# Half-chunk conversion in the first dense layer of a fused attention, expert and dense kernel, with four smaller reorderings

## The chip, the cores and the metric

The program runs on one core of a Trainium2 chip. Its engines are TensorE (PE: matrix products, PEld: their weight loads), VectorE (DVE), ScalarE (ACT), GpSimd (POOL) and SyncE (SP, which here only issues transfers). The metric is the device time of one launch in microseconds (us); lower is better.

## The reference

q, k and v have the shape (4, 12, 448, 64). Three layers follow one another; `x` between them has 1792 rows of 768 numbers.

```python
scores = q @ k.T / sqrt(64) - log(448);  x = sigmoid(scores) @ v    # attention, then heads side by side
e = argmax(x @ w_gate, axis=1)                                      # 8 experts, one for each row
out[e == i] = gate[e == i] * (relu(x[e == i] @ w1[i]) @ w2[i])      # 768 -> 1024 -> 768
h = relu(out @ w_in);  result = (h * h) @ w_out                     # dense: 768 -> 2048 -> 768
```

`w_in` and `w_out` come as float64. The kernel turns them into float32 itself, with integer operations on the two 32-bit words of each number.

## The kernel before

Every float32 product is made of three products of rounded parts: a high part (ACT copies it into a rounding type) and a low part (DVE subtracts), high times high, high times low, low times high. So each weight or operand tile costs one ACT and one DVE pass before PE can use it (`split_w`, L498 and L499; `stage_high` and `stage_low`, L640 and L643; `halves`, L1110 and L1111).

The instruction order is written by hand: inside `tc.manual_schedule()` every engine runs its instructions in program order, and an instruction that waits holds back all that stand behind it on its engine. SP's transfers, which also carry all loads, stand in one such order as well.

The stages, in order of time:

- **Attention** over 24 pairs of heads, with the routing of the rows (logits, largest expert) beside it.
- **15 slots** of 128 rows each, all of one expert. `make_slot` gives `up(c)` for c = 0..3 and `down(c)` for c = 4..7, one for each weight chunk of 128x1536 numbers. After each, `next_chunk(s, c)` splits that chunk for the next slot and loads the one after. Slots 0 and 1 use the same expert, found early. The other rows' places are worked out in slot 0 by `opening(c)`: `late_places` (DVE, at c = 4) computes each row's place and then the one-hot tables `Bs` and `Bt` (L279, L281); `spots` (DVE, c = 5, 16 instructions, L223) builds `A`. In slot 1, `pick_rows` (16 small PE products, L227) multiplies both, and `late_rows` writes the row numbers by which GpSimd gathers rows. `xtrans` (c = 5 of each slot, L307 to L309) transposes the next slot's rows and splits them into `xh` and `xl`.
- **First dense layer, block 0** (rows 0 to 1023, in halves h of 512): `layer1(c, h)` for 8 chunks c, 36 PE products of 512 columns each (L1204 to L1206), in two groups `fi` of 18. ACT evicts a group by `r` (Relu, L1210) and squares it into `h` (L1213); there are two PSUM buffers. Between them `rest()` is called four times in each step (k == 2 of a group, and after it). It works through `todo`: the float64 conversion of the dense weights' chunks 9 to 15, 8 calls each. `narrow(n, step, ...)`: step 0 loads a chunk (1536 KB, L103); steps 1 to 4 are four DVE instructions over 128x1536 (L115, L117, L121, L125) and one ACT Abs (L123), which overwrites a word that the DVE instructions of steps 1 and 2 read; then the result goes to `t_d` in DRAM (L129) and the next chunk is loaded; steps 5 and 6 form four sums of 128x384 (L134 to L138) and store them (L139). When a chunk is done, `ready` lets `load_next` read `t_d` back. After steps (0, 0) and (1, 0), `trans_y` transposes the four row tiles of the second half (12 PE transposes after each, L689) out of buffers that `load_y` fills (`yn`, L666); there are two buffers, so the loads of tiles 2 and 3 go out when tiles 0 and 1 have been read. Between the steps stand the weights' splits (`advance`), `second` and `combine` (DVE sums L1218, L1219, L1075 to L1078).
- **Second dense layer, block 0**, as seven products of half-size blocks (L1383 to L1385).
- **Block 1** (rows 1024 to 1791, 768 of them): its first layer is `strassen_in`, 4 column pairs `cp` of 7 products `i` by 2 columns `ci`, 9 PE instructions each (L1267). Products of i = 0 and 1 add into one PSUM bank, as do 2 and 3, and 4 to 6; DVE or ACT reads the bank in between (L1275, L1279, L1281). The operands of i = 4, 5, 6 (blocks 6, 5 and 7) are split late, by `split_late(b)`, in the first column pair. Its second layer is again seven products; `evac` (L1359) adds the results and calls `scatter` (L1174), which writes 128 rows of the output by an indirect transfer from GpSimd. The last three scatters stand behind the loops.

Of the kernel before, what the change touches and what calls it, by code (L numbers as in the profile page):

```python
# [11 lines left out]
F32R = mybir.dt.float32r  # L12
# [3 lines left out]
U32 = mybir.dt.uint32  # L16
# [49 lines left out]
def moe_kernel(ctx: ExitStack, tc: tile.TileContext, qk, v, wg, wm, w2, out):  # L66
# [148 lines left out]
    def places(n):  # L215
        V.tensor_reduce(out=pos[:, :n], in_=posA[:, :, :n].rearrange("p e t -> p t e"), op=ALU.add, axis=AX.X)
        V.tensor_scalar(posi[:, :n], pos[:, :n], 1.0, None, op0=ALU.subtract)
        V.tensor_scalar(sli[:, :n], posi[:, :n], 7, None, op0=ALU.arith_shift_right)
        V.scalar_tensor_tensor(plf[:, :n], sli[:, :n], -128.0, pos[:, :n], op0=ALU.mult, op1=ALU.add)

    def spots(ts):
        for t in ts:
            V.tensor_scalar(A[:, t], iot1[:CP], plf[:, t:t + 1], None, op0=ALU.is_equal)  # L223
# [45 lines left out]
    def late_places(pn, prk):  # L269
        V.tensor_copy(sa[:, 2, 1:], pn)  # L270
        V.scalar_tensor_tensor(dlt, qs[:, :E], -128.0 * LSLOT, sx[:, 0, 1:], op0=ALU.add, op1=ALU.add)
        V.scalar_tensor_tensor(oh2, prk, 0.0, oh, op0=ALU.is_ge, op1=ALU.mult)
        V.scalar_tensor_tensor(posA, Sx[:CP].unsqueeze(2).to_broadcast([CP, E, NR]), 1.0, prk, op0=ALU.add, op1=ALU.add)
        V.tensor_tensor(posB, prk, sa[:CP, 0, 1:].unsqueeze(2).to_broadcast([CP, E, NR]), op=ALU.is_ge)
        V.tensor_tensor(posB, posB, dlt[:CP].unsqueeze(2).to_broadcast([CP, E, NR]), op=ALU.mult)
        V.tensor_tensor(posA, posA, posB, op=ALU.subtract)
        V.tensor_tensor(posA, posA, oh2, op=ALU.mult)
        places(NR)
        V.tensor_tensor(Bs, iot[:CP, :LC].unsqueeze(1).to_broadcast([CP, NR, LC]),  # L279
                        sli.unsqueeze(2).to_broadcast([CP, NR, LC]), op=ALU.is_equal)  # L280
        V.tensor_tensor(Bt, Bs, tokc.unsqueeze(2).to_broadcast([CP, NR, LC]), op=ALU.mult)  # L281
# [364 lines left out]

    ready = [PRE]
    cv = []
    todo = [(n, k) for n in range(PRE, 16) for k in range(1, 9)]

    def rest():
        if not todo:
            return
        n, step = todo.pop(0)
        if step < 7:
            narrow(n, step, *cv, None)
        if step == 4 and n < 15:
            narrow(n + 1, 0, cv[0], None, None)
        if step == 6:
            ready[0] = n + 1  # L660
            load_next()

# [40 lines left out]
    with ExitStack() as mctx:  # L703
# [42 lines left out]
        def make_slot(s, xh, xl, weights):  # L746
            hr = {}
            hh = mp.tile([128, KF, 128], F32R, tag="hh", name=f"hh_{s}", bufs=1)
            hl = mp.tile([128, KF, 128], F32R, tag="hl", name=f"hl_{s}", bufs=1)
            y = mp.tile([128, DM + 1], F32, tag="y", name=f"y_{s}", bufs=1)  # L750
            ps = {}

            def htrans(i):
                pt = ps_ht.tile([128, 4, 128], F32, tag="pht", name=f"pht_{s}_{i}")
                for f in range(4):
                    nc.tensor.transpose(pt[:, f, :], hr[i][:, f * 128:(f + 1) * 128], ident)
                nc.scalar.activation(hh[:, 4 * i:4 * i + 4], pt, AF.Copy)
                nc.vector.tensor_tensor(hl[:, 4 * i:4 * i + 4], pt, f32(hh[:, 4 * i:4 * i + 4]), op=ALU.subtract)

            def up(c):  # L760
                i = c // 2
                if c % 2 == 0:
                    ps[i] = ps_h.tile([128, 512], F32, tag=f"ph{i}", name=f"ph_{s}_{i}")
                w, wl_ = weights(c)
                passes(ps[i], c % 2 == 0, c % 2 == 1, ((0, 0), (1, 0), (0, 1)), 3,
                       lambda a, q: (xh, xl)[a][:, 3 * (c % 2) + q, :], lambda a, q: (w, wl_)[a][:, q * 512:q * 512 + 512],
                       (lambda: htrans(0)) if c == 2 else None)
                if c % 2 == 1:
                    hr[i] = mp.tile([128, 512], F32, tag="hr", name=f"hr_{s}_{i}", bufs=1)
                    nc.scalar.activation(hr[i], ps[i], AF.Relu)  # L770

            def down(c):
                fg, dh = (c - 4) // 2, c % 2
                if fg == 0:
                    ps[2 + dh] = ps_y.tile([128, 512], F32, tag=f"py{dh}", name=f"py_{s}_{dh}")
                w, wl_ = weights(c)
                py = ps[2 + dh][:, :384]
                passes(py, fg == 0, fg == 1, ((0, 0), (0, 1), (1, 0)), 4,
                       lambda a, q: (hh, hl)[a][:, 4 * fg + q, :], lambda a, q: (w, wl_)[a][:, q * 384:(q + 1) * 384])
                if c == 4:  # L780
                    htrans(1)

            def fin(c):
                if c > 5:
                    dh = c % 2
                    nc.scalar.activation(y[:, dh * 384:(dh + 1) * 384], ps[2 + dh][:, :384], AF.Copy, scale=gts[:, s:s + 1])
                if c == 7:
                    nc.gpsimd.tensor_copy(y[:, DM:].bitcast(U32), tok[:, s:s + 1])
                    nc.sync.dma_start(out=y_d[ds(regr[s], 128), :DM + 1] if s >= FS else y_d[128 * s:128 * s + 128, :DM + 1], in_=y)

            return up, down, fin


# [149 lines left out]
        def opening(c):  # L943
            if c == 0:
                take(4)
            elif c == 1:
                counts(pn2, prk2, NR)
                slots(pn2)
                regs(FS)
                regs(FS + 1)  # L950
                for k in (0, 1, 6, 7):
                    reload(FS, k)
            elif c == 2:
                take(5)
                take(6)
            elif c == 3:
                for k in range(2, 5):
                    reload(FS, k)
            elif c == 4:
                take(7)  # L960
                reload(FS, 5)
                late_places(pn2, prk2)
            elif c == 5:
                spots(range(NR))

        r2 = ps_q.tile([128, 512], F32, tag="q", name="r2")
# [2 lines left out]
        for s in range(NBASE):  # L969
# [10 lines left out]
                ycur.append([load_y(0, 0, t, mp.tile([128, CH], F32, tag="qraw", name=f"yr{t}", bufs=QB)[:, :DM + 1], None) for t in range(2)])  # L980
            for c in range(4):
                up(c)
                if s == 1 and c == 0:
                    pick_rows(pr2, Bt, NR)
                    late_rows(pr2)
                    for k in range(FS, FS + 2):
                        xg[k] = gather(k)
                if s == 0:
                    opening(c)
                else:  # L990
                    next_chunk(s, c)
                if s == 1 and c == 2:
                    late_sums()
                if s == FS:
                    if c == 2:
                        late_gates()
                    if c == 3:
                        more = nc.values_load(ctl[0:1, 2, NBASE:NBASE + 1], min_val=0, max_val=NT)
                q_step(s, c)
                if last:  # L1000
                    trans_y(0, 0, c, ycur[0][c], ynext, ps_x, ("px0", "px1"))
            if last:
                cv.extend(wpair(w, F32, f"{w}c") for w in ("wh", "wl"))
                narrow(PRE, 0, cv[0], None, None)
                start_ring()
            for c in range(4, 8):
                down(c)
# [147 lines left out]
        V.tensor_tensor(t3, t2, h0, op=ALU.subtract)  # L1155
        V.tensor_tensor(t3, t3, l0, op=ALU.subtract)

    def split_late(b):
        k2 = page(F32R, f"x{b}k")[:, :2 * DH]
        X[b] = [[page(F32R, f"x{b}{n}")[:, :2 * DH], k2[:, i * DH:(i + 1) * DH]] for i, n in enumerate("hl")]  # L1160
        for t in range(3):
            halves(X[b], t, late[b][t].rearrange("p (k n) -> p k n", k=3))

    def operand(b):
# [2 lines left out]
    def advance():  # L1167
        used[0] += 1
        if pos_["s"] < len(seq):
            stage(pos_["s"])  # L1170
            load_next()

    def scatter(t, ob):
        return nc.gpsimd.indirect_dma_start(out=out[:, :], out_offset=bass.IndirectOffsetOnAxis(ap=idx2[:, t:t + 1], axis=0),  # L1174
                                            in_=ob, in_offset=None)

    def quarter_rows():
        for q in range(NQ):
# [7 lines left out]
    for bi, (t0, P) in enumerate(blocks):  # L1186
# [47 lines left out]
        def strassen_in():  # L1234
# [18 lines left out]
            for cp in range(4):  # L1253
                bank = {}
                for i, o in enumerate(TURN):
                    for ci in range(2):
# [25 lines left out]
                            nc.scalar.activation(h[end], h[end], AF.Relu)  # L1282
                        if end is not None:
                            nc.scalar.activation(h[end], h[end], AF.Square)
                        if cp == 0 and (i, ci) in ((0, 1), (1, 0), (1, 1)):
                            split_late({1: 6, 2: 5, 3: 7}[2 * i + ci])
                        if (i, ci) == (0, 1) and held:
                            stage_high(held.pop())
                            late_low = True
# [127 lines left out]
                    if i < 4:  # L1417
                        parts.append(load_part((i + 2) % 3, (i + 2) // 3))
    order.close()
    sent = []  # L1420
    for p in range(P):
        st = scatter(t0 + p, obs[0][p])
        for other in sent:
            tc.declare_no_dep(st.ins, other, reason="every scatter writes rows of its own")
        sent.append(st.ins)


def layout(q, k, v, moe_w_gate, moe_w1, moe_w2, moe2_w_in, moe2_w_out):
# [45 lines left out]
```

## Time and profile before

| what | value |
|---|---|
| device time, median of 3 runs | 940.14 us (939.84 to 940.34) |
| the profiled execution's own time | 940.25 us |
| its span, first to last instruction | 938.8 us |
| mean granted TensorE clock over the span | 0.994 |
| PE, DVE, ACT, POOL busy, share of the span | 98%, 73%, 60%, 10% |

Busy means that an instruction of the engine was under way. The time is about 1.45 us more than the span. [...]

### The profile page before, as it was taken

To read this page: it belongs to the slowest core of one execution; us is meant where nothing else is said; L and a number is where in the kernel's file an instruction comes from. 1 tells how busy PE (TensorE), PEld (TensorE's weight loads), DVE (VectorE), ACT (ScalarE), POOL (GpSimd) and SP (SyncE) were. 2 spreads that over 40 slices of the span, in tenths; PEclk is the share of its full clock that TensorE was granted. 3 is DMA by queue.
4 is the path that set the end of the run, shared out by engine and by line. 5 is a ranking of instruction groups with operands and counts; after the bars stand their busy time and mean duration, and the time that the engine had idled before them with its cause. 6 is when DMAs were issued, how large, how long until landed. Compare 5 with 4: busy or idle time off the path is not lost. (4 is left out here: it accounts for less than half of the span.)

```text
span 938.8 us, 15174 instructions
## 1 busy us (share of the span) xinstructions
PE 922.3 (98%) x5803; PEld 774.7 (83%) x5803; DVE 689.8 (73%) x821; ACT 567.2 (60%) x704; POOL 98.5 (10%) x132
## 2 busy tenths in 40 slices
PE   9999999999999999999998999999999999999997
PEld 4555555589888888889987878889999999999997
DVE  3888876689876867768856797847878766569863
ACT  5767755758777777777854345445544456666541
POOL 1000001111311110101001111110000220000002
PEclk9999999999999999999999999999999999999999
DMA  8798977681787969692536787664333345456412
GB/s 289 261 368 319 336 240 247 211 312 46 247 296 266 371 242 365 231 402 98 213 148 237 268 298 245 230 251 135 103 118 118 119 158 195 135 172 236 130 35 101
DMA packets 62753, 206.36 MB, mean 220 GB/s; under 512 B 9106, under 2 KB 28690, under 8 KB 60626
## 3 DMA queue, kind: packets, MB, share of 16 engines
q1 hardware_dynamic: 42562, 159.85, 48.9%
q0 software_dynamic: 8816, 39.73, 10.9%
q10 hardware_dynamic: 11296, 5.75, 2.2%
q8 instruction: 47, 0.77, 0.3%
q14 instruction: 32, 0.26, 0.1%
HBM read 210.40 MB, written 45.63 MB: 273 GB/s over the span
## 5 line engine op out<-in xcount | busy, mean ns | idle before, releaser
L499 DVE TENSOR_TENSOR wl<-raw,wh 128x1536 fp32r<-128x1536 f32 x109 | 190.0, 1756 | 56.7 <-ACT wh L498 54.0
L498 ACT ACTIVATE wh<-raw 128x1536 fp32r<-128x1536 f32 x109 | 160.1, 1482 | 2.2 <-PE ph L732 1.9
L396 ACT ACTIVATE a<-sc,bias_s 128x896 f32<-128x896 f32 x96 | 82.6, 913 | 55.7 <-PE sc L392 55.7
L1383 PE MATMUL pq<-wrh,sh 128*128 128x384 f32 x264 | 89.0, 337 | 0.0
L1385 PE MATMUL pq<-wrh,sl 128*128 128x384 f32 x264 | 88.8, 336 | 0.0
L1384 PE MATMUL pq<-wrl,sh 128*128 128x384 f32 x264 | 88.7, 336 | 0.0
L499 DVE TENSOR_TENSOR wrl<-raw,wrh 128x1536 fp32r<-128x1536 f32 x25 | 43.8, 1756 | 22.3 <-ACT wrh L498 22.3
L498 ACT ACTIVATE wrh<-raw 128x1536 fp32r<-128x1536 f32 x25 | 37.0, 1483 | 38.2 <-PE pq L1385 38.2
L402 PE MATMUL po<-a,qkv 128*64 128x448 f32 x288 | 59.6, 548 | 0.0
L732 PE MATMUL py<-wh,hh 128*128 128x384 f32 x240 | 55.4, 352 | 0.0
L1231 DVE TENSOR_TENSOR sl<-h,sh 128x1024 fp32r<-128x1024 f32 (+1 forms) x47 | 51.6, 1111 | 4.2 <-ACT sh L1230 4.2
L732 PE MATMUL ph<-wh,xh 128*128 128x512 f32 x180 | 53.4, 405 | 0.0
L732 PE MATMUL ph<-wl,xh 128*128 128x512 f32 x180 | 52.9, 402 | 0.0
L732 PE MATMUL ph<-wh,xl 128*128 128x512 f32 x180 | 51.7, 396 | 0.8 <-DVE xl L309 0.8
L732 PE MATMUL py<-wh,hl 128*128 128x384 f32 x240 | 51.7, 337 | 0.0
L732 PE MATMUL py<-wl,hh 128*128 128x384 f32 x240 | 51.6, 336 | 0.0
L1210 ACT ACTIVATE r<-pp 128x512 f32<-128x512 f32 x32 | 19.2, 600 | 51.4 <-PE pp L1206 51.4
L1385 PEld LDWEIGHTS pq<-wrh,sl 128*128 128x128 f32 x264 | 49.5, 188 | 0.3 <-DVE sl L1231 0.3
L1384 PEld LDWEIGHTS pq<-wrl,sh 128*128 128x128 f32 x264 | 49.5, 188 | 0.0
L1383 PEld LDWEIGHTS pq<-wrh,sh 128*128 128x128 f32 x264 | 49.5, 188 | 0.0
L1230 ACT ACTIVATE sh<-h 128x1024 fp32r<-128x1024 f32 (+1 forms) x47 | 44.5, 962 | 7.6 <-PE pq L1384 6.7
L402 PEld LDWEIGHTS po<-a,qkv 128*64 128x64 f32 x288 | 18.4, 136 | 32.7 <-issue 30.6
(447 smaller groups left out, 2156.5 us busy)
## 6 DMA issues: line engine op xcount, KB each, us to landing
raw<-in_wm SPq DMA_DIRECT2D x110, 768.0 KB
qraw<-in_wm SPq DMA_DIRECT2D x32, 768.0 KB
raw<-t_d SPq DMA_DIRECT2D x28, 768.0 KB
cs<-in_w SPq DMA_DIRECT2D x9, 1536.0 KB
qkv<-in_qk SPq DMA_DIRECT2D x23, 480.0 KB
whc<-in_w SPq DMA_DIRECT2D x7, 1536.0 KB
t_d<-wlc POOLq DMA_DIRECT2D x14, 768.0 KB, 8.6
qkv<-in_v SPq DMA_DIRECT2D x24, 256.0 KB
```

The lines of the kernel that those rows point to most:

```text
L396: nc.scalar.activation(a[:, :n], ps[:, :n, :S], AF.Sigmoid, bias=bias_s, scale=1.0 / math.sqrt(D))
L402: nc.tensor.matmul(po[64 * h:64 * h + 64, :S], vr[:, 128 * c + 64 * h:128 * c + 64 * h + 64], a[:, h], start=(c == 0), stop=False, skip_gr ...
L498: nc.scalar.activation(h, src, AF.Copy)
L499: nc.vector.tensor_tensor(l, src, f32(h), op=ALU.subtract)
L732: nc.tensor.matmul(ps, left(i, q), right(j, q), start=first and a == 0 and q == 0, stop=last and a == 2 and q == n - 1)
L1210: nc.scalar.activation(r[:, :N], pp[:, :N], AF.Relu)
L1230: nc.scalar.activation(sh[:, :2 * N], src, AF.Copy)
L1231: V.tensor_tensor(sl[:, :2 * N], src, f32(sh[:, :2 * N]), op=ALU.subtract)
L1383: nc.tensor.matmul(po[p][:, :DH], lh, wc[:, w0:w0 + DH], start=(q == 0 and kk == 0 and o in (0, 2, 5)), stop=False, **fl)
L1384: nc.tensor.matmul(po[p][:, :DH], lh, wcl[:, w0:w0 + DH], start=False, stop=False, **fl)
L1385: nc.tensor.matmul(po[p][:, :DH], ll, wc[:, w0:w0 + DH], start=False, stop=(q == 3 and kk == 1), **fl)
```

## The change

- **Conversion.** `todo` has steps 0 to 7 for each chunk. Steps 0 to 2 convert the first half of the chunk's columns (768 results), 4 to 6 the second half; 3 does nothing. Step 0 or 4 issues the first two DVE instructions of a half, 1 or 5 the third and the Abs, 2 or 6 the fourth; after that the half goes to `t_d` and the same half of the next chunk is loaded (768 KB). Step 7 issues all four sums and their store, and raises `ready`. The loads of chunk 9 are two halves too.
- **Routing.** `Bs` and `Bt` move out of `late_places` into `late_picks`, which stands at c = 5 of slot 0, behind `xtrans` and ahead of `spots`. `pick_rows`, `late_rows` and two gathers move from behind `up(0)` of slot 1 to behind `up(1)`; `next_chunk(1, 0)` moves there as well. `up(0)` of slot 1 multiplies by the weights' low part second and by `xl` third; before it was the other way round.
- **Late split.** `split_late(7)` was called once, at (i, ci) = (1, 1). Now its three tiles are split one each at (2, 0), (2, 1) and (3, 0).
- **Last scatters.** Each of the last three scatters is declared independent of the three scatters before it; before, only of each other.

```diff
@@ late_places
         places(NR)
+
+    def late_picks():
         V.tensor_tensor(Bs, iot[:CP, :LC].unsqueeze(1).to_broadcast([CP, NR, LC]),
...
@@ the conversion
-    todo = [(n, k) for n in range(PRE, 16) for k in range(1, 9)]
+    todo = [(n, k) for n in range(PRE, 16) for k in range(8)]
+    HC = CH // 2
+
+    def fetch_half(n, hf):
+        src, c = cv[0], slice(hf * HC, hf * HC + HC)
+        if wide:
+            nc.sync.dma_start(out=src[:, hf * CH:hf * CH + CH].bitcast(U32), in_=w2[:, n, c].bitcast(U32))
...
+    def narrow_half(n, hf, step):
+        src, c = cv[0], slice(hf * HC, hf * HC + HC)
+        raw_ = cv[1][:, c]
+        if wide:
+            pairs = src[:, hf * CH:hf * CH + CH].rearrange("p (n two) -> p n two", two=2)
+            lo_u, hi_u = pairs[:, :, 0].bitcast(U32), pairs[:, :, 1].bitcast(U32)
+            du = raw_.bitcast(U32)
+            if step == 0:
+                nc.vector.tensor_scalar(du, hi_u, 3, 0x3FFFFFF8, op0=ALU.logical_shift_left, op1=ALU.bitwise_and)
+                nc.vector.scalar_tensor_tensor(du, hi_u, 0xC0000000, du, op0=ALU.bitwise_and, op1=ALU.bitwise_or)
+            elif step == 1:
+                nc.vector.scalar_tensor_tensor(du, lo_u, 29, du, op0=ALU.logical_shift_right, op1=ALU.bitwise_or)
+                nc.scalar.activation(pairs[:, :, 1], pairs[:, :, 1], AF.Abs)
+            else:
+                nc.vector.scalar_tensor_tensor(raw_, pairs[:, :, 1], TINY, raw_, op0=ALU.is_ge, op1=ALU.mult)
...
+        if step == 2:
+            nc.gpsimd.dma_start(out=t_d[2 * hf:2 * hf + 2, :, n - 8, :].rearrange("s p c -> p s c"), in_=raw_.rearrange("p (s c) -> p s c", s=2))
+            if n < 15:
+                fetch_half(n + 1, hf)
@@ rest
-        if step < 7:
-            narrow(n, step, *cv, None)
-        if step == 4 and n < 15:
-            narrow(n + 1, 0, cv[0], None, None)
-        if step == 6:
+        if step % 4 < 3:
+            narrow_half(n, step // 4, step % 4)
+        if step == 7:
+            for k in (5, 6):
+                narrow(n, k, *cv, None)
             ready[0] = n + 1
             load_next()
@@ up
-                passes(ps[i], c % 2 == 0, c % 2 == 1, ((0, 0), (1, 0), (0, 1)), 3,
+                passes(ps[i], c % 2 == 0, c % 2 == 1, ((0, 0), (0, 1), (1, 0)) if (s, c) == (1, 0) else ((0, 0), (1, 0), (0, 1)), 3,
@@ opening, the slots' loop
             elif c == 5:
+                late_picks()
                 spots(range(NR))
...
-                if s == 1 and c == 0:
+                if s == 1 and c == 1:
                     pick_rows(pr2, Bt, NR)
                     late_rows(pr2)
...
-                else:
+                elif (s, c) != (1, 0):
+                    if (s, c) == (1, 1):
+                        next_chunk(1, 0)
                     next_chunk(s, c)
...
-                narrow(PRE, 0, cv[0], None, None)
+                fetch_half(PRE, 0)
+                fetch_half(PRE, 1)
@@ strassen_in
-                        if cp == 0 and (i, ci) in ((0, 1), (1, 0), (1, 1)):
-                            split_late({1: 6, 2: 5, 3: 7}[2 * i + ci])
+                        if cp == 0 and (i, ci) in ((0, 1), (1, 0)):
+                            split_late(6 if i == 0 else 5)
+                        if cp == 0 and 4 <= 2 * i + ci < 7:
+                            split_late(7, (2 * i + ci - 4,))
@@ the last scatters (every scatter is now put into sent)
-        for other in sent:
+        for other in sent[-P - 1:-1]:
             tc.declare_no_dep(st.ins, other, reason="every scatter writes rows of its own")
```

## Rows read from the trace of the kernel before

**Rows 1.** PE's waits over the span: us in total, times, longest.
```profile
PE pyt L689 <- DMA yn<-y_d: 3.4, 2, 1.8
...
PE pp L1204 <- ACT r L1210: 0.8, 1, 0.8
```
**Rows 2.** PE's timeline in the dense layer: start, us, instruction, count [idle before].
```profile
499.12 1.47 PE L689 MATMUL pyt<-ident,yn 128*128 128x128 f32 x12
500.34 0.48 PE L1204 MATMUL pp<-yt,wrh 128*128 128x512 f32 x1
...
508.40 0.39 PE L1206 MATMUL pp<-yt,wrl 128*128 128x512 f32 x1
...
514.22 0.78 PE L1204 MATMUL pp<-yt,rh 128*128 128x512 f32 x1
...
524.78 0.40 PE L1204 MATMUL pp<-hy,wrh 128*128 128x512 f32 x1
```
**Rows 3.** Busy time by stretch: PE, PEld, DVE, ACT, POOL, clock, DMA share, GB/s.
```profile
514.00:516.00 2.00, 2.00 (x7) 1.69 (x6) 0.95 (x3) 1.04 (x3) 0.00 (x0) 0.50 0.98 403
```
**Rows 4.** SP's timeline, 484 to 520: transfers issued.
```profile
500.44 0.33 SPq L103 DMA_DIRECT2D whc<-in_w  x1
500.95 2.04 SPq L666 DMA_DIRECT2D yn<-y_d  x2
```
**Rows 5.** DVE's groups, 490 to 625, by shape: count, busy us, mean ns.
```profile
L117 DVE SCALAR_TENSOR_TENSOR wlc<-whc,wlc 128x1536 uint32<-128x1536 uint32 x7 | 12.3, 1759 | 0.2
...
L115 DVE TENSOR_SCALAR wlc<-whc 128x1536 uint32<-128x1536 uint32 x7 | 6.7, 954 | 0.8 <-DMA t_d<-wlc 0.8
...
L134 DVE TENSOR_TENSOR wlc<-wlc 128x384 f32<-128x384 f32 x7 | 3.9, 555 | 0.1
```
**Rows 6.** ACT's timeline, 529 to 570.
```profile
560.82 1.64 ACT L123 ACTIVATE whc<-whc 128x1536 f32<-128x1536 f32 x1 [5.50 <-DVE wlc L117]
```
**Rows 7.** PE's timeline at the start of slot 1.
```profile
198.17 0.85 PE L732 MATMUL ph<-wh,xh 128*128 128x512 f32 x3
199.80 0.97 PE L732 MATMUL ph<-wh,xl 128*128 128x512 f32 x3 [0.78 <-DVE xl L309]
...
204.95 0.86 PE L732 MATMUL ph<-wh,xh 128*128 128x512 f32 x3
```
**Rows 8.** DVE's timeline around the start of slot 1.
```profile
198.00 0.55 DVE L279 TENSOR_TENSOR Bs<-iot,sli 112x384 f16<-112x384 f16 x1
...
199.06 1.02 DVE L309 TENSOR_TENSOR xl<-px,xh 128x512 fp32r<-128x512 f32 x2
199.99 2.68 DVE L223 TENSOR_SCALAR big<-iot,plf 112x128 f16<-112x128 f16 x16
```
**Rows 9.** DVE's timeline late in slot 1.
```profile
217.47 1.02 DVE L309 TENSOR_TENSOR xl<-px,xh 128x512 fp32r<-128x512 f32 x2
```
**Rows 10.** PE's timeline at the start of slot 2.
```profile
219.84 0.86 PE L732 MATMUL ph<-wh,xl 128*128 128x512 f32 x3
```
**Rows 11.** PE's timeline in block 1's first layer.
```profile
763.15 0.69 PE L1267 MATMUL pi<-xw,rl 128*128 128x384 f32 x3
765.54 0.62 PE L1267 MATMUL pi<-xw,rh 128*128 128x384 f32 x2 [1.70 <-DVE h L1279]
```
**Rows 12.** DVE's timeline there.
```profile
764.94 1.02 DVE L1279 TENSOR_TENSOR h<-pi,h 128x384 f32<-128x384 f32 x2
```
**Rows 13.** ACT's timeline there.
```profile
762.89 0.40 ACT L1110 ACTIVATE x7h<-tm 128x256 fp32r<-128x256 f32 x1
...
764.41 1.47 ACT L640 ACTIVATE wrh<-raw 128x1536 fp32r<-128x1536 f32 x1
```
**Rows 14.** POOL's timeline at the end.
```profile
927.66 0.96 POOL L1174 DMA_INDIRECT out<-ob,idx  x1 [3.60 <-issue]
...
933.99 0.96 POOL L1174 DMA_INDIRECT out<-ob,idx  x1 [0.30 <-issue]
```
**Rows 15.** DVE's timeline at the end.
```profile
932.18 0.56 DVE L1359 TENSOR_TENSOR ob<-pq,ob 128x384 f32<-128x384 f32 x1 [3.61 <-PE pq L1385]
```

More of the change, by code (lines that the diff above doesn't have):

```diff
@@ L648, in moe_kernel @@
     cv = []
-    todo = [(n, k) for n in range(PRE, 16) for k in range(1, 9)]
+    todo = [(n, k) for n in range(PRE, 16) for k in range(8)]
[5 more added lines that the diff above has]
+        else:
+            nc.sync.dma_start(out=src[:, c], in_=w2[:, n, c])
+    def narrow_half(n, hf, step):
[11 more added lines that the diff above has]
+                nc.scalar.activation(pairs[:, :, 1], pairs[:, :, 1], AF.Abs)
+            else:
+                nc.vector.scalar_tensor_tensor(raw_, pairs[:, :, 1], TINY, raw_, op0=ALU.is_ge, op1=ALU.mult)
+        elif step == 0:
+            nc.vector.tensor_copy(raw_, src[:, c])
+        if step == 2:
+            nc.gpsimd.dma_start(out=t_d[2 * hf:2 * hf + 2, :, n - 8, :].rearrange("s p c -> p s c"), in_=raw_.rearrange("p (s c) -> p s c", s=2))
+            if n < 15:
+                fetch_half(n + 1, hf)
     def rest():
@@ L1156, in part_b, with split_late @@
         V.tensor_tensor(t3, t3, l0, op=ALU.subtract)
[L1158 to L1161, printed above, removed]
+    def split_late(b, ts=range(3)):
+        if 0 in ts:
+            k2 = page(F32R, f"x{b}k")[:, :2 * DH]
+            X[b] = [[page(F32R, f"x{b}{n}")[:, :2 * DH], k2[:, i * DH:(i + 1) * DH]] for i, n in enumerate("hl")]
+        for t in ts:
             halves(X[b], t, late[b][t].rearrange("p (k n) -> p k n", k=3))
@@ L1171, in advance @@
             load_next()
+    sent = []
     def scatter(t, ob):
-        return nc.gpsimd.indirect_dma_start(out=out[:, :], out_offset=bass.IndirectOffsetOnAxis(ap=idx2[:, t:t + 1], axis=0),
-                                            in_=ob, in_offset=None)
+        st = nc.gpsimd.indirect_dma_start(out=out[:, :], out_offset=bass.IndirectOffsetOnAxis(ap=idx2[:, t:t + 1], axis=0),
+                                          in_=ob, in_offset=None)
+        sent.append(st.ins)
+        return st
     def quarter_rows():
@@ L1419, in moe_kernel @@
     order.close()
-    sent = []
     for p in range(P):
         st = scatter(t0 + p, obs[0][p])
-        for other in sent:
+        for other in sent[-P - 1:-1]:
             tc.declare_no_dep(st.ins, other, reason="every scatter writes rows of its own")
-        sent.append(st.ins)
 def layout(q, k, v, moe_w_gate, moe_w1, moe_w2, moe2_w_in, moe2_w_out):
```

## The prediction

> **What bounds the kernel now.** I read the page first, then PE's waits over the span, then the stages in which a wait stands. PE is busy for 98% of the span, so the change can win only where PE stands still, where it runs at the lower clock, or behind its last product. PE's waits [rows 1] are short: 3.4 us in two pieces for `yn`, 0.8 us for an eviction `r`, and two that the timelines show in place: 0.8 us for `xl` [rows 7] and 1.7 us for an `h` [rows 11]. Around the longest, the reader should compare two steps of the dense layer. In the step that begins at 500.34 the 36th product starts at 508.40, so 36 products take 8.06/35 x 36 = 8.29 us. The step after it should begin when that step and 12 transposes are through: 508.40 + 0.23 + (500.34 - 499.12) = 509.85. [...] So one late transfer costs 524.78 - (509.85 + 8.29) = 6.6 us, 4.4 as waiting and 2.3 as clock, about twice what the list of waits shows. Last comes the tail: three scatters that go out after the last product [rows 14, 15].
>
> **Conversion in halves: why `yn` comes in time.** SP sends the next chunk's load, 1536 KB, at 500.44, and the two `yn` loads (384 KB each) stand behind it, from 500.95 on; the second goes out at 500.95 + 2.04 - 0.33 = 502.66 [rows 4]. It has landed when the second six transposes run, about 514.22 - 1.2 = 513.0. So SP moved 2304 KB in 12.6 us beside POOL's 768 KB store, 183 KB/us. With the change only the first half of the next chunk stands ahead: 768 KB, so 1536 KB with both `yn`. It also leaves earlier. The whole chunk's four DVE instructions take 0.95 + 3 x 1.76 = 6.2 us [rows 5] and the load leaves behind the fourth. A half takes between 0.55 (the 384-column row) and 1.76 us an instruction; by the straight line through 384 and 1536 columns it is 0.95 us, and 0.55 for the first: 3.4 us for a half. Its Abs stands on ACT behind an `r` and an `h`, so I put the first half's load at 498.3, not 497.6. At 183 KB/us the last `yn` has landed by 498.3 + 8.4 = 506.7; PE wants tile 2 at 508.63 and tile 3 at 509.2. It arrives 2.5 us early, and would be late below 1536 / 10.9 = 141 KB/us. Then neither the wait nor the slow clock remains: **-6.6 us**. The next transfer on SP, the second half's, is issued a step later, behind both `yn`.
>
> [...]
>
> **Does DVE stay quick enough?** The 0.8 us wait for `r` [rows 1] comes from a stretch in which DVE has no pause: an Abs on ACT waits 5.50 us for DVE (560.82), and the eviction `r` stands behind it [rows 6]. Ahead of that Abs, DVE will have done one chunk in halves (+0.6 us) and two half instructions in place of two whole ones (1.5 in place of 2.7 us), and the Abs itself is half as long (-0.8 us). The `r` comes 1.4 us earlier, more than the 0.8 us that PE waits: **-0.8 us** (bounds 0 and -0.8). The removed PE pause takes no time from DVE: there it waited for `yn` as well, and what is left over after two steps is done beside the third. Step 7 issues four sums at once (4 x 0.55 us), which no engine but POOL waits for. `ready` rises two calls (about 4 us) later in each chunk; only the last matters, and the part of `t_d` that is read back first comes from the first half, which is stored a step earlier.
>
> **Routing.** `xl` stands behind `Bs` and `Bt`, which take from 198.00 to 199.06 [rows 8]. Without them it ends at about 199.0. With the new order of passes PE wants it 2 x 0.7 us after 198.17, at 199.6: the 0.8 us wait goes. DVE's work up to the last spot is the same, to 199.99 + 2.68 = 202.67 [rows 8]. Before, the picks stood in front of `up(1)` and waited for it; now PE does both `up` first, to 198.17 + 18 x 0.23 = 202.3, and the picks end with the last spot at about 202.9. `up(2)` begins there instead of at 204.95 [rows 7]: 2.05 us at most. What is late next: the chunk splits for slot 2 go out one `up` later and DVE is full there. Its `xl` for slot 2 ends at 217.47 + 1.02 = 218.49 and is wanted at 219.84 [rows 9, 10], so 1.35 us are safe even if DVE gains nothing. I take the middle: **-1.7 us** (bounds -1.3 and -2.05). The gathers behind the picks go out at about the same time as before, and SP's reload of the first chunk is a step later with a slot's time to land.
>
> **Late split.** The product at 765.54 waits 1.70 us for the `h` of 764.94, which stands behind the whole split of block 7 [rows 11, 12]. Without it PE goes on at 763.15 + 3 x 0.17 = 763.67 (384 columns, three quarters of 0.23): 1.87 us at most. But the second of the two `h` now stands behind the first tile, and that tile's ACT half stands behind a weight split that was behind all three: six ACT instructions from 762.89, then 1.47 us from 764.41 [rows 13]. Moved up it ends at 764.4, the first tile's ACT part (1.52/3 = 0.5) at 764.9, its DVE part, taken as long, at 765.4, `h` at 765.9. The products that wait for it ran at 765.54 + 9 x 0.17 = 767.1 and will run at 765.95: **-1.15 us** (bounds -0.2, if DVE is later still, and -1.87). The other two tiles lie under products that do not need them yet.
>
> **Last scatters.** The last one's data is ready at 932.18 + 0.56 = 932.74 [rows 15]. It goes out at 933.99, since the chain behind the scatter of 927.66 is late: each waits for the landing of the one before [rows 14]. Freed, the two before it go out behind that one, by 928.6 + 2 x 1.26 = 931.1 (0.96 each and 0.30 between, as at 933.99), so the last goes out with its data: **-1.2 us** (bounds -0.6, if POOL is held once more, and -1.25). Everything behind it moves along.
>
> **Sum.** -6.6 - 0.8 - 1.7 - 1.15 - 1.2 = -11.45. From the profiled execution's own 940.25 us that is 928.8; the runs' median, 940.14, is 0.11 below it, so a median of 928.7 to 928.8. The bounds together (6.1 to 6.8 for the first, since a step of 36 products may be 0.2 us faster or 0.5 slower) give 927.7 to 932.
>
> **Rivals.**
> - *`yn` still comes late* (POOL's half store and the first half's load slow it below 141 KB/us). For it: the DMA engines were 0.98 busy at 403 GB/s in that stretch [rows 3], with more than SP's bytes on them. Against: 2.5 us to spare. If tile 3 is 2 us late, the pause and part of the slow clock, some 4.3 us, remain: 933.1. Chance 0.13. [...]
> - *Routing and late split are given back* further on, since DVE and ACT are full in those stretches; only conversion and scatters stay: 940.25 - 8.6 = 931.7. Chance 0.12.
> - *The end of the conversion blocks ACT*: `ready` late by two calls, the read of `t_d` late, ACT held at the next weight split and the evictions behind it. Price 4.1 us or more: 933. Chance 0.05.
> - *Slower: halves cost nearly what wholes cost on DVE.* At 1.76 us a half a chunk takes 12.5 instead of 6.2 us of DVE. In the stretch without a pause, two and a half chunks long, that is 15.7 us, 14 beyond the 1.4 us of room: 943. It decides from about 5.2 us more a chunk, a half instruction at 1.6 us. Against: the rows at 384 and 1536 columns. Chance 0.05.
> - *The halves change nothing* (a half waits for the other, and nothing leaves earlier), and the rest about cancels: within 0.2%, 939.5. Chance 0.03.
>
> **How the numbers follow.** The forecast has the remaining 0.62: 928.8, its own range 927.7 to 931.5. The range for 8 in 10 reaches to the first two rivals and, for a PE rate a little better than I took, below the forecast's own: 927.0 to 933.5. A difference of 0.2%, 1.9 us, is about what a measurement of this kernel can tell from no change; with that bound the cases give faster 0.92, same 0.03, slower 0.05.
>
> **What would show it.** No PE wait for `yn`, and a granted clock of 1.00 from the first product to the last: else the first step is wrong. The half load before 499 and `yn` landed before 508. DVE instructions over 768 columns at 0.95 us. No PE wait for `r`. `up(2)` of slot 1 begins 4.7 to 5.4 us after `up(0)`, instead of 6.8. At most 0.9 us of PE wait for an `h` in block 1. The last scatter within 0.1 us of its data. A new wait of PE for an eviction in the dense layer would make the prediction wrong.

## The result and the profile after

The changed kernel takes 929.58 us (median of 4 runs, 928.85 to 930.01) against 940.14 us (939.84 to 940.34): ratio 0.9893, 95% interval 0.9878 to 0.9908. The profiled execution took 928.85 us, its span is 927.4 us and its mean granted clock, a share of full speed, 0.998 (before 0.994). In 5 of 25 further runs the kernel before took 936.7 to 937.0 us; the last section comes back to this.

PE's waits over the span, us in total, times, longest:

```profile
PE pw L459 <- DVE rest_t L456: 1.7, 1, 1.7
PE pp L1245 <- ACTq L1071: 0.7, 1, 0.7
...
PE pi L1308 <- DVE h L1320: 0.4, 1, 0.4
PE pht L788 <- ACT hr L802: 0.2, 1, 0.2
```

The first two stand in the list of the kernel before too, with the same 1.7 and 0.7 us. `yn`, the eviction `r` and `xl` are gone; `h` has shrunk from 1.7 to 0.4 us, and a small new one has come, for `hr` (the hidden rows of an expert, which PE transposes in a slot). PE's timeline in the dense layer (start, us, instruction, count):

```profile
496.73 1.47 PE L721 MATMUL pyt<-ident,yn 128*128 128x128 f32 x12
497.95 0.48 PE L1245 MATMUL pp<-yt,wrh 128*128 128x512 f32 x1
...
506.25 1.47 PE L721 MATMUL pyt<-ident,yn 128*128 128x128 f32 x12
507.47 0.48 PE L1245 MATMUL pp<-yt,rh 128*128 128x512 f32 x1
...
515.96 0.40 PE L1245 MATMUL pp<-hy,wrh 128*128 128x512 f32 x1
```

All twelve transposes of a pair of row tiles stand in one row with no idle time ahead of them, and the step that took 10.56 us at the lower clock [rows 2] takes 515.96 - 507.47 = 8.49. The windows there (PE, PEld, DVE, ACT, POOL busy; clock; DMA share; GB/s) show a granted clock of 1.00 throughout, where [rows 3] showed 0.50. The mean is not 1.000 because the clock falls behind PE's last product (0.50 from 924 to 927):

```profile
500.00:508.00 8.00, 8.00 (x43) 6.78 (x42) 7.34 (x15) 4.32 (x8) 1.59 (x3) 1.00 0.86 280
508.00:516.00 8.00, 8.00 (x36) 6.40 (x35) 6.96 (x18) 2.90 (x8) 2.14 (x4) 1.00 0.94 355
```

SP's timeline there, to set beside [rows 4]:

```profile
495.92 0.33 SPq L657 DMA_DIRECT2D whc<-in_w  x1
497.57 3.03 SPq L698 DMA_DIRECT2D yn<-y_d  x2
```

DVE's groups between 480 and 615 by shape (count, busy us, mean ns), beside [rows 5]:

```profile
L670 DVE SCALAR_TENSOR_TENSOR wlc<-whc,wlc 128x768 uint32<-128x768 uint32 x14 | 13.4, 958 | 0.5
...
L669 DVE TENSOR_SCALAR wlc<-whc 128x768 uint32<-128x768 uint32 x14 | 7.8, 554 | 0.0
```

To see where the 11.4 us of span went I cut PE's timeline at the first PE instruction of each stage, in both traces. Each number is the difference of two such starts:

| stage on PE | before | after | other |
|---|---|---|---|
| program start to slot 0 | 179.57 | 178.82 | -0.75, unchanged code |
| slots 0 and 1 | 39.58 | 37.49 | -2.09 |
| slot 2 | 18.88 | 18.88 | 0 |
| slots 3 to 14 | 252.77 | 253.22 | +0.45 |
| dense layer to its 4th step (first `hy`) | 33.98 | 27.55 | -6.43 |
| rest of the dense layer | 108.27 | 107.39 | -0.88 |
| second dense layer, block 0 | 121.22 | 121.22 | 0 |
| block 1, first layer | 89.86 | 88.61 | -1.25 |
| block 1, second layer | 87.68 | 87.70 | +0.02 |
| last PE instruction to the end | 6.99 | 6.52 | -0.47 |

### The profile page after: what moved, and what is told of

Read it like the earlier page. It is cut to its first block, busy times and chain, and to the rows that moved or that the text cites. A ratio compares the mean times of both kernels' runs of the same rounds, so it can differ in the third digit from the quotient of the medians.

```text
span 927.4 us, 15244 instructions
## 1 busy us (share of the span) xinstructions
PE 917.4 (99%) x5803; PEld 771.8 (83%) x5803; DVE 692.6 (75%) x849; ACT 567.5 (61%) x711; POOL 101.0 (11%) x139
```

## The experiments

These stages are used below as well, since they tell more than a total that differs by some 0.1% from run to run. The first four kernels ran beside a kernel before of 940.34 us (939.24 to 940.87).

**order_only.** Is it the halves, or only that a smaller load stands ahead of `yn`? The kernel before, with chunk 10's whole load issued one call later, behind `yn`:

```diff
-        if step == 4 and n < 15:
+        if n < 15 and step == (5 if n == PRE else 4):
```

> The kernel before with one edit: the load of chunk 10 (whole, 1536 KB) is issued one call later, behind the two yn loads instead of ahead of them; conversion stays in whole chunks. Theory (order): the 6.6 us went to yn standing behind a whole chunk on SP, so this alone gives it: about 933.6, no wait of PE for yn, granted clock 1.00 until the last product; the 0.8 us wait for an eviction stays. Rival (halves): the gain needs the finer DVE and ACT steps; then this gives less than 2 us, 938 or more, because PE meets other waits in the same place.

936.41 us (934.94 to 936.84), ratio 0.9956 (0.9939 to 0.9972). No wait for `yn` and no stretch at the lower clock: the stage falls to 27.55, the whole 6.43 us. But the rest of the dense layer goes from 108.27 to 110.63, and PE waits for `r` 2.8 us in three places instead of 0.8 in one. Its ACT timeline shows why:

```profile
521.53 1.67 ACT L123 ACTIVATE whc<-whc 128x1536 f32<-128x1536 f32 x1 [5.46 <-DVE wlc L117]
538.82 1.67 ACT L123 ACTIVATE whc<-whc 128x1536 f32<-128x1536 f32 x1 [5.25 <-DVE wlc L117]
557.13 1.73 ACT L123 ACTIVATE whc<-whc 128x1536 f32<-128x1536 f32 x1 [6.35 <-DVE wlc L117]
```

ACT stands three times for over 5 us at an Abs, with PE's evictions queued behind it. In the kernel before the Abs of these three chunks waited 0, 3.66 and 5.50 us. Two things stand behind this. DVE's rows at the start of chunk 10, in order_only and then in the kernel before, show them:

```profile
518.75 0.96 DVE L115 TENSOR_SCALAR wlc<-whc 128x1536 uint32<-128x1536 uint32 x1 [2.65 <-DMA whc<-in_w]
```
```profile
518.14 0.95 DVE L115 TENSOR_SCALAR wlc<-whc 128x1536 uint32<-128x1536 uint32 x1
```

The first is this edit's own doing: DVE waits 2.65 us for the whole load that now leaves at 507.05 instead of 500.44, and the 0.58 us that PE first waits for `r` stands behind that. At the next chunk DVE waits again, 1.41 us, for the store of chunk 10's sums. The second is the lost pause. From the dense layer's first product on, DVE reaches this row after 518.75 - 2.65 - 491.26 = 24.84 us, without the wait for the load; before it was 518.14 - 490.80 = 27.34. DVE is 2.5 us earlier where PE is 6.43 earlier, so PE's pause had let DVE catch up by some 3.9 us. How the lost 2.36 us divide between the late load and the missing pause no run here separates.

**conversion_only.** The kernel before with the conversion's part of the change alone.

> The kernel before with the conversion in halves alone; routing, late split and last scatters as before. Theory: -6.4 to -7.4, about 933 (no yn wait, no wait for r, clock 1.00). Rival (parts lean on one another): less than 5 us, because the DVE work that the other edits moved still stands in the way.

932.15 us (931.67 to 933.06), ratio 0.9919 (0.9902 to 0.9935). The stage takes 27.55, the rest 107.34; PE waits neither for `yn` nor for `r`, and its waits for `h` (1.7) and `xl` (0.9) are about as before. Against order_only the halves are worth 110.63 - 107.34 = 3.29 us behind the stage; in this sum stand shorter instructions and loads of which DVE needs only a half at a time.

**other_three.** The changed kernel with the conversion's part of the change undone.

> The changed kernel with the conversion undone: routing, late split and last scatters alone. Theory: 2.1 + 1.25 + 0.5 = 3.85 less than before, about 936.3, with the yn wait of 3.4 us and the slow clock as before. Rival (given back): what PE wins in slot 1 it loses behind it, since DVE is full there; 938 or more.

936.05 us (935.25 to 936.46), ratio 0.9958 (0.9942 to 0.9975). The late `yn` is back, in PE's timeline and in the windows:

```profile
508.26 0.84 PE L691 MATMUL pyt<-ident,yn 128*128 128x128 f32 x6 [1.64 <-DMA yn<-y_d]
510.96 1.51 PE L691 MATMUL pyt<-ident,yn 128*128 128x128 f32 x6 [1.85 <-DMA yn<-y_d]
```
```profile
511.00:512.00 1.00, 1.00 (x5) 1.00 (x6) 0.04 (x1) 0.00 (x0) 0.00 (x0) 0.50 1.02 425
```

By totals the two parts give 940.34 - 932.15 = 8.2 and 940.34 - 936.05 = 4.3 us, together 12.5, but whole_load, below, which has both, gives 10.8. The stages show 1.05 of the 1.7 us too much: here the `yn` stage takes 32.93 us, not the 33.98 of before, with a shorter stretch at the lower clock (0.88 by the window from 514 to 515), so a part of the clock's loss is missing in this run and counts twice in the sum. Elsewhere the parts do not touch: slots 0 and 1 take 37.52, slots 3 to 14 253.18, block 1's first layer 88.57.

**whole_load.** Half instructions, but both half loads of the next chunk go out together, behind the second half's work:

```diff
-            if n < 15:
-                fetch_half(n + 1, hf)
+            if n < 15 and hf == 1:
+                fetch_half(n + 1, 0)
+                fetch_half(n + 1, 1)
```

> The changed kernel with DVE and ACT in halves, but the next chunk's two half loads both issued behind the second half's work. Theory (order): nothing stands ahead of yn any more, so no yn wait; the next chunk's load leaves about 507 and lands before DVE wants it at 514: 929.6, within 1 us of the changed kernel. Rival (the half loads are needed to feed DVE): DVE waits for the load at each chunk, the evictions come late, 931 to 935.

929.57 us (928.73 to 930.55), ratio 0.9891 (0.9875 to 0.9908); the stages are 27.56 and 107.30, the waits those of the changed kernel. Sending the first half load earlier adds nothing here (27.55 and 107.39 in the changed kernel): behind the second half's work the load is behind `yn` too. The two halves leave at 504.49 and some 2.8 us later, about as late in the layer as order_only's whole load, and PE waits for no `r` behind them.

**load_ahead_768, load_ahead_1536.** How early is `yn`? The changed kernel, with one or two idle copies of 768 KB (from the weights into an unused array in DRAM) ahead of the `yn` loads on SP:

```diff
+            if n == PRE and hf == 0:
+                for i in range(1):      # and range(2)
+                    nc.sync.dma_start(out=j_d[:, i * CH:(i + 1) * CH].bitcast(U32), in_=w2[:, i, :HC].bitcast(U32))
```

> The changed kernel with one more transfer on SP: 768 KB, read from the weights and written to a scratch array in DRAM that nothing reads, right behind the first half load of chunk 10 and ahead of both yn loads. Theory: SP moves some 183 KB/us there, so the last yn lands about 12.6 us after 495.9, at 508.5, where PE wants it at 506.8; a wait for yn of 1 to 2 us comes back, and if the clock falls behind it 2 us more: 1 to 4 us over the changed kernel. Rival (there is far more room than 2.5 us): no wait at all, same time.

> The same with twice 768 KB. Theory: the last yn lands about 16.8 us after 495.9, at 512.7: a wait of 5 to 6 us in two pieces and the granted clock at 0.50 behind it, 7 to 9 us over the changed kernel. Rival (more room): at most the 3.4 us of wait of the kernel before.

One run each, beside 940.2 us. With one copy 928.84 us, no wait for `yn`, the stage 27.55: another 768 KB cost nothing. That makes 1536 KB ahead of `yn`, as many as in the kernel before, so half the bytes were not needed; the queue starts some 2 us earlier in the layer here, and half of POOL's store runs beside it. With two 931.63 us, the stage 29.60 (+2.05), and PE's timeline:

```profile
508.10 0.85 PE L725 MATMUL pyt<-ident,yn 128*128 128x128 f32 x6 [0.81 <-DMA yn<-y_d]
509.81 0.85 PE L725 MATMUL pyt<-ident,yn 128*128 128x128 f32 x6 [0.86 <-DMA yn<-y_d]
```

There SP's 3072 KB, sent from 496.78 on, had landed by 509.81: 236 KB/us, not the 183 that I read from before (the copies go from DRAM to DRAM, so the mix of transfers is not the same). The granted clock stayed at 1.00 behind these two pauses (windows from 509 to 515).

**dve_dose.** Is the halves' cost on DVE, which the prediction feared, near the bound? The fourth DVE instruction of each half is issued twice (14 x 0.96 us more).

```diff
+                for _ in range(2):
                     nc.vector.scalar_tensor_tensor(raw_, pairs[:, :, 1], TINY, raw_, op0=ALU.is_ge, op1=ALU.mult)
```

> The changed kernel with the fourth DVE instruction of each half issued twice (the second leaves the same values): 14 instructions of 0.96 us more. Theory: in the stretch where DVE has no pause (about 526 to 565) two of them stand ahead of the Abs that holds back an eviction, which had under half a microsecond of room: PE waits for r come back, 1.5 to 4 us in all, 931 to 934. Rival (DVE is not near being the bound): PE waits for no r, time as in the changed kernel.

934.16 us (933.98 to 934.28), ratio 0.9939 (0.9916 to 0.9961). The stage keeps 27.55; the rest takes 111.57, 4.2 us more, with 3.7 us of PE waiting for `r` in two places. A chunk costs DVE 1.9 us more here. So the changed kernel has little room left. Its own longest wait of an Abs is

```profile
551.75 0.93 ACT L673 ACTIVATE whc<-whc 128x768 f32<-128x768 f32 x1 [5.25 <-DVE wlc L670]
552.56 0.59 ACT L1251 ACTIVATE r<-pp 128x512 f32<-128x512 f32 x1
```

Its 5.25 us are almost as long as the 5.50 of [rows 6], but the Abs takes 0.93 instead of 1.64 us and PE does not wait for the `r` behind it.

**picks_early.** Are later picks needed, or only later one-hots? The changed kernel with `pick_rows` and what follows it behind `up(0)` again.

```diff
-                if s == 1 and c == 1:
+                if s == 1 and c == 0:
                     pick_rows(pr2, Bt, NR)
```

> The changed kernel with the picks, the row numbers and the two gathers back behind up(0) of slot 1; Bs and Bt stay behind xl, and the next chunk's split stays at up(1). Theory: the spots end at the same time as ever, so PE, which no longer waits for xl, now waits for the spots at the picks: slot 1 takes about 2 us more than in the changed kernel (20.9 instead of 18.9 us from its start to slot 2's), so taking Bs and Bt out of xl's way gains nothing by itself. Rival: moving Bs and Bt is what gives the 2.1 us; then slot 1 stays at 18.9 to 19.4.

932.19 us (one run). Slots 0 and 1 take 41.11 us: 3.6 more than in the changed kernel, and 1.5 more than before. PE's timeline, then the window behind:

```profile
198.76 0.86 PE L764 MATMUL ph<-wh,xl 128*128 128x512 f32 x3
199.50 2.62 PE L227 MATMUL r<-Bt,big 112*128 112x24 f16 x16
201.97 0.94 PE L764 MATMUL ph<-wh,xh 128*128 128x512 f32 x3
```
```profile
203.00:206.00 3.00, 3.00 (x9) 2.32 (x8) 0.00 (x0) 0.66 (x2) 1.54 (x2) 0.51 1.02 420
```

The sixteen small products now take 2.62 us, each behind its spot on DVE, instead of 0.56; then the granted clock is 0.51, from 203 to 206. The two moves belong together.

**slot1_pass_order.** The changed kernel with `xl` second again in slot 1's first unit.

> The changed kernel with slot 1's first unit in the old order of passes, xl as the second operand before wl. Theory of the prediction, where the later one-hots alone free xl in time: the first part of xl starts at 197.23 and takes 0.51 us, so it is there at 197.8, before the second pass at 198.12; no wait, 929.6, and the new order is a cover that is not used. Rival: xl's second part and its semaphore are needed by the second pass, PE waits 0.2 to 0.6 us for xl there, and slot 0 and 1 take 37.7 to 38.1 us instead of 37.49.

929.88 us (one run); slots 0 and 1 take 37.51, no wait for `xl`. The later one-hots alone remove that wait.

**scatters_waiting.** The changed kernel with the old dependence of the last scatters.

> The changed kernel with the last scatters waiting for each other as before. Theory after the result: the waits cost 0.48 us at the end (the last scatter starts 1.25 us after its data instead of 0.77), the time from the last PE instruction to the end of the span is 7.0 us instead of 6.52, and the total is 930.0. Rival, the prediction's: the waits cost 1.2 us, the tail is 7.7 us and the total 930.8; its 0.5 us on the changed kernel's side would then be something else that came in with the change.

930.19 us (one run). POOL's timeline:

```profile
921.40 0.96 POOL L1211 DMA_INDIRECT out<-ob,idx  x1 [2.91 <-DMA out<-ob,idx]
922.66 0.96 POOL L1211 DMA_INDIRECT out<-ob,idx  x1 [0.30 <-DVE ob L1398]
923.93 0.96 POOL L1211 DMA_INDIRECT out<-ob,idx  x1 [0.30 <-issue]
```

Its last data is ready on DVE at 922.03 + 0.56 = 922.59, so the last scatter starts 1.34 us behind it, as before (1.25). From the last PE instruction to the end are 928.7 - 921.65 = 7.05 us instead of 6.52: the change gives some 0.5 us, not the prediction's 1.2.

**split_later.** The changed kernel with the three pieces of block 7's split one product later.

```diff
-                        if cp == 0 and 4 <= 2 * i + ci < 7:
-                            split_late(7, (2 * i + ci - 4,))
+                        if cp == 0 and 5 <= 2 * i + ci < 8:
+                            split_late(7, (2 * i + ci - 5,))
```

> The changed kernel with the three pieces of the late split one product later each, nothing else. Theory: the wait of 0.4 us for h in block 1 is the last piece standing ahead of it on VectorE, so it goes, the stage from the first pi to the second pq takes 88.2 us instead of 88.61, and the time is 929.2. Rival: the wait is for the products that h is made of, it stays at 0.4 us, and the pieces, now 1 us later, are late for the product that reads them, which shows as a wait at a second place.

928.47 us (one run). The stage takes 88.39 instead of 88.61: half of what I expected. The wait at the old place is gone, but DVE now runs two `h` behind a weight's split, and PE waits there, 4 us later (DVE's row, then PE's):

```profile
759.84 1.02 DVE L1322 TENSOR_TENSOR h<-pi,h 128x384 f32<-128x384 f32 x2
```
```profile
760.54 0.59 PE L1308 MATMUL pi<-x5h,wrh 128*128 128x384 f32 x2 [0.29 <-DVE h L1322]
```

So neither theory is quite right: the wait was queue order, and half of it only moves.

**gates_first.** split_later, with slot 2's gate products (they give `gts`, the gate values by which ACT scales the rows `y` of an expert's result) ahead of slot 3's transposes, and slot 3's first unit using `xh` twice before `xl`:

```diff
+                if s == FS and c == 5:
+                    gates()
                 if c == 5 and s + 1 < NBASE:
                     xs[s + 1] = xtrans(s + 1, xg.pop(s + 1), pxt(s + 1))
```

> The changed kernel with the two waits that it still has behind its own parts taken out: the second dense layer's split pieces stand one product later, so that the first h of block 1 is not queued behind the last of them, and slot 2's gate products and their three VectorE reads stand ahead of slot 3's transposes, with slot 3's first unit using xh before xl, as slot 1's does. Theory: both waits are queue order alone. The h wait of 0.4 us goes, the stage from the first pi to the second pq falls from 88.61 to 88.2, ScalarE's y of slot 2 waits 2.6 us again instead of 3.3 or less, the hr wait of 0.2 goes, slot 3 falls from 22.78 to 22.33 us, and the time is 928.7 against 929.6 for the changed kernel. Rival: the room that routing gained was no real room, slot 3's xl or the hidden rows come late by as much as the gates come early, and the time stays at 929.6.

928.77 us (927.91 to 929.41, 6 runs), ratio 0.9893 (0.9874 to 0.9913) beside 939.59. In its ACT timeline the wait for the gates is 1.81 us where the changed kernel had 3.29:

```profile
235.41 0.58 ACT L818 ACTIVATE y<-py,gts 128x384 f32<-128x384 f32 x1 [1.81 <-DVE gts L957]
```

The wait for `hr` is gone, and slots 3 to 14 take 252.77 again: the 0.45 us that routing had given back was this order, the gates' and the passes' together. By stages the version is 0.45 + 0.22 = 0.67 us faster than the changed kernel. The totals (928.77 and 929.58, not from the same chip) agree with that but cannot show it.

## Why the prediction was right, and where it was not

The forecast of 928.8 us stands beside a profiled 928.85 and a median of 929.58. Term by term, from the table of stages:

| term | predicted | measured |
|---|---|---|
| `yn` in time, with the clock | -6.6 | -6.43 |
| wait for `r` | -0.8 | -0.88 |
| routing | -1.7 | -2.09 + 0.45 = -1.64 |
| late split | -1.15 | -1.25 |
| last scatters | -1.2 | -0.47 |
| program start, not touched | 0 | -0.75 |

Two errors of 0.7 us cancelled in the profiled execution. The start is chance: in the fourteen traces, all with the same code there, it took 178.62 to 180.07, in scatters_waiting 179.66 and in slot1_pass_order 179.92. Without it the changed kernel's profiled run would be 929.6, which is the median. So the agreement to 0.05 us is luck; the sum itself was 0.8 us too hopeful, nearly all of it in the last scatters. The bounds that I named add up to 12.77 us at the most, which makes the lower end 927.5, not 927.7.

**`yn` in time: right; its margin too small.** Of the 6.6 us I called 4.4 waiting (514.22 - 509.85) and 2.3 clock (524.78 - 514.22 = 10.56 us for the step behind, instead of 8.29 [rows 2], at a granted clock of 0.50 [rows 3]). The waits are 3.4 [rows 1]; some 3.2 are the clock, which was down before the second six transposes ran (1.51 us instead of 0.85, as in other_three's rows). The first half's load left at 495.92; PE reached the dense layer 490.80 - 488.41 = 2.39 us earlier, so in the time of before that is 498.31, and I had 498.3. The step that failed is the rate. I took SP's 183 KB/us from a stretch in which POOL stored 768 KB beside it, and set it against one with a half store; load_ahead_1536 has 236 KB/us. That the store makes the difference is not shown. `yn` comes in time with twice as much in front of it (load_ahead_768), so the rival "`yn` still late" was further away than the 0.13 I gave it.

**The wait for `r`: right in size, wrong in a sentence.** I wrote that the removed pause takes no time from DVE. order_only contradicts it: there PE comes 6.43 us earlier and DVE only 2.5, so DVE loses 3.9, and with whole instructions and a later load PE loses 2.36 us behind the stage. With halves it does not. A half costs DVE 554 ns once and 958 ns three times, as the straight line through the rows at 384 and 1536 columns gave (0.55 and 0.95 us). So a chunk in halves takes 2 x (0.554 + 3 x 0.958) = 6.86 us, a whole one 0.954 + 3 x 1.759 = 6.23 [rows 5]: 0.6 us a chunk more, and the changed kernel covers it without a wait for `r`. dve_dose shows that 1.9 us a chunk more would not be covered.

**Routing: right.** `up(2)` began 202.04 - 197.43 = 4.61 us after `up(0)`, a little earlier than the 4.7 to 5.4 that I named. I had taken 1.7 as the middle between 1.3 and 2.05; the gain in the slots was 2.09, the whole, and the loss came elsewhere, so that the net met the forecast to 0.06 us is in part luck. The rival "given back further on" held for 0.45 us of 2.09, by a path that I had not named: PE had become 2.84 us earlier at slot 3 and the gates only 2.2. The row in the changed kernel's ACT timeline:

```profile
235.94 0.58 ACT L818 ACTIVATE y<-py,gts 128x384 f32<-128x384 f32 x1 [3.29 <-DVE gts L957]
```

**Late split: right**, to 0.1 us, as is the mechanism: the second `h` stands behind the first piece.

```profile
755.54 0.55 DVE L1320 TENSOR_TENSOR h<-pi,h 128x384 f32<-128x384 f32 x1
```

**Last scatters: the mis-sized term.** I wrote that the last one goes out with its data, within 0.1 us. POOL's timeline has

```profile
918.43 0.96 POOL L1213 DMA_INDIRECT out<-ob,idx  x1 [1.21 <-DVE ob L1402]
922.59 0.96 POOL L1213 DMA_INDIRECT out<-ob,idx  x1 [3.20 <-issue]
```

and DVE's

```profile
917.10 0.56 DVE L1402 TENSOR_TENSOR ob<-pq,ob 128x384 f32<-128x384 f32 x1 [3.60 <-PE pq L1428]
921.26 0.56 DVE L1402 TENSOR_TENSOR ob<-pq,ob 128x384 f32<-128x384 f32 x1 [3.60 <-PE pq L1428]
```

The data is ready at 917.66 and 921.82, and both scatters start 0.77 us later. The wait removed was 1.25 - 0.77 = 0.48 us. What lies in the 0.77 us no run here took apart. I had also read [rows 14] as if each scatter waited for the landing of the one before. Of the last three only the first did, at 931.46; the other two followed it after 0.30 us of idle time each, and this small queue is what put the last one at 933.99.

## What to carry to other kernels

Price a late transfer by the stage and not by the list of waits: 3.4 us of waiting for `yn` cost 6.4 us, with the granted clock at 0.50 behind the pauses, from 512 to 518. Before removing a pause, ask which engine was catching up in it, and before moving a load back, ask who waits for it: moving the whole load alone won 6.4 us and lost 2.4, for both reasons, and with loads and work in halves nothing was lost. When a stage becomes faster, look at what is next in time for the stage behind it (here the gates, 0.45 us), and let no operation start "with its data" unless a row shows one that does.

## What the hardware showed that I had not expected

- Not every pause was followed by a lower clock. The kernel before was run 25 times beside the experiments: in 20 runs it took 939.2 to 941.0 us at a mean clock of 0.994 to 0.996, in 5 runs 936.7 to 937.0 at 0.999. The windows of the profile of before, which with 940.25 us and 0.994 is like the 20, show 0.50 from 512 to 518 us and 0.80 from 518 to 520:

```profile
512.00:515.00 3.00, 1.94 (x8) 1.88 (x9) 1.22 (x4) 1.04 (x3) 0.00 (x0) 0.50 1.02 422
515.00:518.00 3.00, 3.00 (x8) 2.32 (x8) 2.51 (x7) 0.66 (x2) 0.42 (x1) 0.50 0.37 149
518.00:520.00 2.00, 2.00 (x8) 1.58 (x8) 1.97 (x3) 0.00 (x0) 0.82 (x2) 0.80 0.70 206
```

  That is 6 us at 0.50 and 2 us at 0.80; if PE's pace goes with the granted clock, 6 x 0.50 + 2 x 0.20 = 3.4 us are lost by this estimate, about the difference. So in the 5 the pauses probably stood without the clock's fall, which no trace here shows; against them the change gains 7 us, not 10.6.
- After the two pauses of 0.81 and 0.86 us in load_ahead_1536 the granted clock stayed at 1.00, and after sixteen small products spread over 2.62 us in picks_early it was 0.51, each in one execution.
- The 0.77 us between a scatter's data and its start stand three times in the changed kernel, but not at every scatter. By the times, the one at 914.27 has them too, behind the `ob` that ended at 912.94 + 0.56 = 913.50:

```profile
912.94 0.56 DVE L1402 TENSOR_TENSOR ob<-pq,ob 128x384 f32<-128x384 f32 x1 [1.86 <-PE pq L1428]
```
```profile
914.27 0.96 POOL L1213 DMA_INDIRECT out<-ob,idx  x1 [1.13 <-issue]
```

  The first of the six, at 908.30, started 0.27 us behind the first `ob`, which began at 907.47 and ended at 908.03. Why the two differ no run here shows.
